# Transposing attention weights in two halves of 64 queries, first rotary sums on TensorE, and a new order, in an attention and gated feed-forward kernel

## The chip, the core and the metric

The kernel runs on one core of a Trainium2 chip. The core has TensorE (PE; its weight loads are listed apart as PEld), VectorE (DVE), ScalarE (ACT), GpSimd (POOL) and SyncE (SP, which only issues DMAs here). The metric is device time of one execution in microseconds.

## The reference

Eight batches of eight heads, 576 positions, head size 64. Queries and keys are rotated by position, softmax attention is formed, the heads are laid side by side (512 channels), and a gated feed-forward follows, whose gate is a causal convolution of five taps:

```python
def rotate(x):
    x1, x2 = (x[..., :half], x[..., half:])
    return np.concatenate([x1 * cos - x2 * sin, x1 * sin + x2 * cos], axis=-1)
q_rot, k_rot = (rotate(q), rotate(k))
scores = scale * np.matmul(q_rot, k_rot.transpose(0, 1, 3, 2))
scores = scores - np.max(scores, axis=-1, keepdims=True)
attn = np.exp(scores)
attn = attn / (np.sum(attn, axis=-1, keepdims=True) + 1e-09)
attn_out = np.matmul(attn, v)
...
for k in range(K):
    gate_pre += conv_w[k][None, None, :] * xp[:, k:k + S, :]
gate = 1.0 / (1.0 + np.exp(-gate_pre))
val = x @ w_val
return (gate * val @ w_out).astype(np.float32)
```

Everything is float32. Products that need full precision are made of three reduced ones (high times high, high times low, low times high), in the type fp32r.

## The kernel before, in words

**A pair of heads** is the unit of attention: 32 pairs, four to a batch. Head 0 lies on partitions 0 to 63, head 1 on 64 to 127. The host hands over each query and key twice, as it is and with its halves swapped. For each pair, `load` (L264) brings both copies (`kin`, `qin`); `rope_mul` (L278) multiplies each by the cosine or sine table (`tab`), `rope_add` (L283) adds them, `qk_hi` (L287) and `qk_lo` (L294) split the sum into a high part and a remainder. Keys are held 640 wide: the last 64 positions stand once more in front, so that a chunk of 128 queries can see its keys starting at either place; that wrapped part is loaded and rotated like the rest.

**Scores.** `s_mm` (L306) makes the scores of a chunk of 128 queries for both heads: twelve matmuls on 64 rows each, alternating between the upper and the lower half of the array's rows. A pair has four such chunks, and a fifth of six matmuls, which holds the last 64 queries of both heads. `s_max` (L323, DVE) takes the row maxima, `s_exp` (L328, ACT) the exponentials and their sums into `p`. Scores lie in `ps_s`, which has two places, one for each head, so that the scores of the next chunk wait for the exponentials of this one.

**Transposes.** For the product with the values, the weights `p` must be turned. `t_mm` (L355) turns, for one chunk and one head, four blocks of 128 x 128 into one bank of 512 columns of `ps_t`: a matmul with the block as the stationary operand and the identity as the moving one (`transpose`, L344). `t_copy` (L380) moves the bank to `pt` on ACT or DVE. That makes eight such banks for a pair, and some smaller ones for the remainders (keys m, h0, h1, hm: nine transposes for a pair). `pv_mm` (L406) and `pv_left` (L416) multiply by the values, into `ps_a`; `x_norm` divides by the sums.

**Feed-forward.** `f_mm` (L499) makes both projections of a batch, spread over the time in which the next batch's attention runs. The four banks of `ps_t` are shared by transposes, products with the values and projections.

**Order.** Nothing is scheduled at run time: `ORDER` lists the jobs one by one, with the engine where there is a choice (V, A, G) and the number of the buffer to use. `Plan.run` checks that no job's inputs change by the order and then issues them, so that each engine has a fixed queue. `FILLS` puts transposes of the identity, whose result nobody reads, at some places of PE's queue. The weights arrive as float64 bits; `decode` (L543) turns them into a high part and a remainder on DVE, early in the run.

Of the kernel before, what the change touches and what calls it, by code (L numbers as in the profile page):

```python
# [34 lines left out]
163 178:0 232 117 161 90 227V 164:10 225V 229G 167:1 299 165:3 168:3 91 120G 166:1 92 179V:1 93:0 169:01 125 131 230 188 94:0 170:2 95:0 182:1 172:0
196:3 171 126 128 174:0 231 173 129G 190:0 305 175:1 183A:1 197A:1 184:1 176:0 96 153 189A 233:10 300V 191A 177 185A 198:3 127 192:2 199A 200:0 234:3
194:1 193A 130G 236:2 235:3 97 237:0 307V 195A 238:10 202:1 306V 203:1 132 205:3 308G 241:0 239:1 259:2 242 180:1 301V 204:1 309 206 181A 310 240
186:1 302V 552 201A 243:01 98 303 275:0 380 187A 304G 244:3 276A:0 207:1 246:2 245:2 208 133 247:1 546 99 248:01 134 381 135 265:0 553G 251:0 209
266A:0 249:1 252 382 250 253:1 554G 210 211 138 261:0 254:3 263:3 262A:0 257:1 548V 255:0 383 258A 555V 273:0 260A 269:1 256 556 547V 312:01 270A 557
264A 267:2 214:1 279:1 549G 315:2 277:3 281:0 313:0 274A 282:0 316:3 271:0 384 631 136 314:0 215 272A 317:10 137 385 216 550 284:0 268A 386G 318:1 285  # L40
320:3 387G 319 286:2 217 388 321 283:0 551V 278A 322:10 212:1 218 280A 287 633G 325:2 625 323:0 326:2 340:3 311 389 324:1 288 390 139V 341A:1 327:01
391 140G 290 336:1 328:1 346:3 392 338:2 329 632V 339A:1 332:0 393 634G 330:3 337A 333:2 331 394 347A 356 627V 350:1 395 357A:1 342:3 626V 334:2 396V
343A 352:2 335 351A 397G 289 559:10 293:2 628V 398 348:3 353A 558 213:1 562:0 354:1 635 358:0 344:2 560:1 563:0 636 629 294 291:2 360:1 345A 399 361:1
400 561:3 585:2 710 401 630V 349A 564:01 355A 402 405 403 363:3 704 295 406G 565:3 364 362:1 292:2 567:2 566 365:1 359V 568 296 587:0 586A:0 569:01
404 588A:0 297 366 711G 570:0 572:1 571:2 583:2 407V 573:1 591:0 712V 408 298 574:01 705V 584A 592A 589:2 706G 575:3 367 577:2 576 716 368 578 579:0
369 707V 370:3 593:0 409 590A 597:3 580:0 371:3 708 601:1 595:2 594V 581:0 603:0 410 596A 709V 638:10 602A:0 604A 411 783 372:3 582 599:2 412 605:1
458:0 413 607:0 373 598A 459 608:0 415 414 460 600A 639:1 416G 606A 610:3 641:3 417G 640:3 612:2 374 418 642:1 713V 219 643:10 375 714 613 609:0 785G
644:2 646:0 645 611 715 647 662:1 419 789 614 376 663A:1 100 648:10 420 421 461:0 668:1 637 422 462 470:0 615 669A:1 463 651:1 464:3 425 423 465 652:2
784G 649:3 466 616 650:0 664:1 467:1 680:2 426V 468 653:01 424 665A 791V 681A:1 670:3 617:4 427G 656:2 476:1 671A 477 469 654:0 428 657 478 790V 655
658:1 619:4 792G 672:2 659:1 674:3 471 479:2 675A 786V 676:1 660:1 666:3 429 673A 717:01 430 661 677A 431 667A 620 678:2 793 682:1 432 684:3 472 683A  # L50
433 679A 720:3 488:1 435 489 718:2 721:3 436G 490 686:1 434 482:2 719:0 687:1 437V 483 794 438 685A 484 480 621 956 722:10 481 491:0 473:1 691:3 618:4
723:0 688:1 725:1 724 741:1 494:0 439 726 622 495 787 440 727:10 441 742A:0 788G 474 689:1 728:3 692 729:2 623 950 957G 730:2 690 485:2 731:1 693 442
486 732:10 445 443 487 694 695 743:2 475 733:0 749:1 744A 444 747:3 446G 735:1 750A 745:2 748A:0 500:1 447V 736 952V 448 751:3 501 746A 951V 737:0 734
958V 752A 496 953G 738:3 377 759:2 761:3 502 760V:0 739:0 497:2 755:2 503:1 762A 753:0 449 954 740 757:1 450 756A 763:3 796:10 451 758A 955V 765:0 498
770:2 452 766:0 698:0 799:2 499 492 797:1 771 800:3 453 959V 798:1 822:1 767:0 754V 764A 801:01 823A:1 699 504 455 768:3 505 804:0 960 1029 802:3 456G
769 805 961 803 772 454 1035 806:10 774 457G 773 777:1 493 838:0 807:2 516:1 809:1 517 808:2 506:2 700 810:0 518 839A:1 1030G 811:10 519A:1 520 824:3
814:0 795 1031G 820:0 812:3 830:1 815 507 821V 825A:1 816:0 1032V 831A 508 1036G 1033 817:2 511:0 509A:2 512 813 510 828:3 1037V 834:1 829A 1034V
826:2 818:1 513 1038G 835V 1108 526:3 827A 963:10 819 1039 840:1 964:1 832:2 514A:0 836:0 841V 833A 527 1040 965:3 528 966:0 1114 847:1 778 967:0 848
837V 1109G 529V:1 968:10 987:2 779 842:0 521:3 843A 1110G 971:3 988A:0 522 969:2 523 972 531:2 524V:2 844:1 1111G 970 532 525 533 845:1 989:0 701 515
849:3 530 990V 702 850 534A:2 846:1 780 703 973:01 1115V 696:0 624 991:0 697:0 974:1 962 775:1 993:2 976:0 851 994A:0 776:1 992V 975:2 536:2 1005:0  # L60
977:1 853 537 1116V 995:3 852 978:01 1117G 996V 854:2 856:2 997:1 979:3 538 1006A:0 855:2 981:2 980 541:3 542 982 857 983:0 539A:0 998V 543 1112 984:1
862:0 544A:1 999:2 1113V 1118 1007:1 863 1000A 858 1187 1001:3 985:0 864 1002A 545 986 1042:10 1119 1008A 1009:2 1043:0 1193 1003:3 1014:1 865:2
1044:3 781 1015 1004A 1010V 1045:3 1011:0 1016:0 1012:0 859 1046:2 535 1017 860 1120 782 1189V 1047:10 1188V 1066:3 1050:2 1190G 1068:2 1067A:1 1048:1
1018 866 1049 1013:0 868:3 1194V 869 1069A 1195G 1051 870 1070:2 1041 861 871:1 1052:10 1071V:1 872 873 1072:3 1053:0 874:2 867 1073A 1055:3 875
1054:1 1196G 1019 1084:3 876 1020 1056:0 1085V:1 1074:1 1023:3 1057:10 1075V 1021:3 877:0 1076:0 1024 880:3 1058:1 881 1060:2 882 1059 886:1 1025
1077A 1062:1 1061 883:1 1026 887 1191 1078:2 1063:0 1197 1080:0 1079V 1086:3 1064:2 888 1027 892:2 884 889:2 1081A 1121:01 1192V 890 1028 1065 1082:1
# [142 lines left out]
def attn_gated_ffn(ctx: ExitStack, tc: tile.TileContext, q2, k2, v2, tab, w_val, conv_w, w_out, out, collect=None):  # L209
# [578 lines left out]
```

## Time and profile before

| | |
|---|---|
| three runs | 743.93, 746.06, 747.79 us |
| the profiled execution | 746.22 us |
| its span in the trace | 744.4 us |
| mean granted clock of PE | 0.993 |
| matmuls | 6047 |
| PE busy, of which transposes (L349) | 718.6 us, 189.7 us |
| scores (L320) | 174.8 us, 1728 matmuls |
| row maxima (L326, DVE), 288 | 208.7 us |
| exponentials (L334, ACT), 288 | 212.7 us |

A group's busy time is the union of its instructions; a matmul's recorded duration runs over that of the next ones, so the step from one start to the next is the cost, not the duration. "Idle before" is the time an engine stood still ahead of these instructions, and behind the arrow stands what ended it.

### The profile page before, as it was taken

The numbers are of one execution on the slowest core, as the hardware profiler recorded it, in microseconds if no ns is written. First come the engines' busy times: TensorE is split into PE (matmuls) and PEld (weight loads), VectorE is DVE, ScalarE is ACT, GpSimd is POOL, SyncE is SP. The second block draws the span as 40 slices with busy tenths as digits, with TensorE's granted clock in tenths as the row PEclk, the third lists the DMA queues.
The fourth block names the chain that finished last, engine by engine and source line by source line (L and its number), as shares of the span: only waits on it lengthen the run. The fifth ranks groups of instructions, "written<-read, shape, count | busy, mean of one in ns | idle before, by whom it ended". The sixth has DMA issues, their size and how long they took to land. (4 is left out here: it accounts for less than half of the span.)

```text
span 744.4 us, 15945 instructions
## 1 busy us (share of the span) xinstructions
PE 718.6 (97%) x6047; PEld 583.5 (78%) x6047; DVE 605.3 (81%) x999; ACT 497.2 (67%) x1159; POOL 306.2 (41%) x234
## 2 busy tenths in 40 slices
PE   9897989999999999999999999999999999999998
PEld 9665656878788787877777887777878878788888
DVE  4999989998988887888888887778887878877741
ACT  1776777878676867667666876676667666776621
POOL 3344243445533614554324553454435353062121
PEclk9999899999999999999999999999999999999999
DMA  6443343234343332243432133433242243311012
GB/s 199 134 151 107 89 143 98 76 101 127 117 135 93 87 120 91 71 122 117 130 104 93 56 111 104 125 95 115 79 121 66 83 145 109 89 53 52 17 49 72
DMA packets 61167, 75.33 MB, mean 101 GB/s; under 512 B 25338, under 2 KB 35619, under 8 KB 61091
## 3 DMA queue, kind: packets, MB, share of 16 engines
q1 hardware_dynamic: 60002, 73.60, 32.6%
q8 instruction: 48, 0.79, 0.4%
q10 hardware_dynamic: 1088, 0.72, 0.4%
q14 instruction: 29, 0.23, 0.1%
HBM read 64.70 MB, written 9.59 MB: 100 GB/s over the span
## 5 line engine op out<-in xcount | busy, mean ns | idle before, releaser
L334 ACT ACTIVATE p<-ps_s,nm 128x576 f32<-128x576 f32 x288 | 212.7, 742 | 109.0 <-DVE nm L326 107.0
L326 DVE TENSOR_REDUCE nm<-ps_s 128x1 f32<-128x576 f32 x288 | 208.7, 750 | 68.8 <-PE ps_s L320 64.4
L349 PE MATMUL ps_t<-ident,p 128*128 128x128 f32 (+1 forms) x1316 | 189.7, 280 | 8.2 <-ACT pt L402 4.4
L320 PE MATMUL ps_s<-k,q 64*128 64x288 f32 (+1 forms) x1728 | 174.8, 309 | 11.4 <-ACT p L334 10.8
L349 PEld LDWEIGHTS ps_t<-ident,p 128*128 128x128 f32 (+1 forms) x1316 | 147.6, 142 | 37.6 <-issue 16.9
L320 PEld LDWEIGHTS ps_s<-k,q 64*128 64x128 f32 (+1 forms) x1728 | 136.7, 185 | 51.1 <-ACT p L334 28.2
L402 ACT COPY pt<-ps_t 128x512 f32<-128x512 f32 x203 | 116.3, 587 | 58.3 <-PE ps_t L349 57.6
L413 PE MATMUL ps_a<-pt,v 128*64 128x256 f32 (+1 forms) x1024 | 136.2, 414 | 0.3 <-ACT pt L402 0.2
L490 DVE SCALAR_TENSOR_TENSOR g<-x,cw,g 128x576 f32<-128x576 f32 (+1 forms) x132 | 118.4, 898 | 2.2 <-ACT g L487 1.5
L513 PE MATMUL ps_f<-y,wout_hi 128*128 128x288 f32 (+2 forms) x512 | 111.1, 303 | 0.0
L413 PEld LDWEIGHTS ps_a<-pt,v 128*64 128x64 f32 x1024 | 70.1, 138 | 49.9 <-issue 7.3
L528 POOL TENSOR_TENSOR y<-y,y 128x288 fp32r<-128x288 f32 (+2 forms) x64 | 56.0, 883 | 111.5 <-ACT y L525 97.4
L513 PEld LDWEIGHTS ps_f<-y,wout_hi 128*128 128x128 f32 x512 | 82.6, 188 | 5.5 <-issue 2.8
L281 POOL TENSOR_TENSOR qin<-qin,tab 128x640 f32<-128x640 f32 (+1 forms) x36 | 58.7, 1638 | 62.9 <-DMA qin<-in_q 60.5
L513 PE MATMUL ps_f<-xh,wval_hi 128*128 128x288 f32 (+2 forms) x256 | 78.2, 307 | 1.3 <-DVE pt L404 0.8
L513 PE MATMUL ps_f<-xl,wval_hi 128*128 128x288 f32 (+2 forms) x256 | 76.5, 301 | 0.0
L513 PE MATMUL ps_f<-xh,wval_lo 128*128 128x288 f32 (+2 forms) x256 | 76.3, 300 | 0.0
L513 PE MATMUL ps_f<-y,wout_lo 128*128 128x288 f32 (+2 forms) x256 | 76.1, 300 | 0.0
L281 POOL TENSOR_TENSOR kin<-kin,tab 128x640 f32<-128x640 f32 (+1 forms) x29 | 49.6, 1721 | 59.0 <-DMA kin<-in_k 58.9
L477 POOL TENSOR_TENSOR xl<-x,xh 128x576 fp32r<-128x576 f32 (+2 forms) x33 | 47.3, 1437 | 45.6 <-ACT xh L471 27.7
L404 DVE COPY pt<-ps_t 128x512 f32<-128x512 f32 x85 | 57.4, 678 | 8.0 <-PE ps_t L349 7.8
L334 ACT ACTIVATION_READ_ACCUMULATOR p<-ps_s,nm 128x1 f32 x288 | 57.2, 199 | 0.0
(70 smaller groups left out, 838.5 us busy)
## 6 DMA issues: line engine op xcount, KB each, us to landing
kin<-in_k SPq DMA_DIRECT2D x31, 576.0 KB
qin<-in_q SPq DMA_DIRECT2D x31, 512.0 KB
v<-in_v SPq DMA_DIRECT2D x32, 320.0 KB
out_t<-o SPq DMA_DIRECT2D x56, 144.0 KB
rb<-rd SPq DMA_DIRECT2D x31, 144.0 KB
rb<-rd SPq DMA_DIRECT2D x31, 128.0 KB
kin<-in_k SPq DMA_DIRECT2D x32, 64.0 KB
wst<-in_w_val SPq DMA_DIRECT2D x4, 512.0 KB
```

Source lines behind the costliest of these rows:

```text
L281: eng.tensor_tensor(out=t[:, i, a:b], in0=t[:, i, a:b], in1=table[:, i, a + at:b + at], op=ALU.mult)
L320: T.matmul(out=tiles[h][:, half, 0:288], lhsT=st["q"][rows, x, c * 128:c * 128 + 128], rhs=st["k"][rows, y, k0:k0 + 288], start=(i == 0), ...
L326: V.tensor_reduce(out=st[f"nm{i}"], in_=st[f"s{i}"], axis=AX.XY, op=ALU.max, negate=True)
L334: A.activation(out=st[f"p{t}"][:, part].rearrange("p (b x) -> p b x", b=2), in_=st[f"s{i}"], func=AF.Exp, bias=st[f"nm{i}"], scale=1.0, ac ...
L349: T.transpose(out=bank[0:src.shape[1], j * 128:(j + 1) * 128], in_=src, identity=ident)
L402: A.copy(out=dst, in_=src)
L404: V.tensor_copy(out=dst, in_=src)
L413: T.matmul(out=st[f"a{g}"][HEAD[h], 0:n], lhsT=st["v"][:, j, h, :], rhs=st[f"pt{g}"][:, h * 4 + j], start=(j == 0), stop=False)
L477: G.tensor_tensor(out=st["xl"][:, a:b], in0=xs[p % 2][:, 4 + a:4 + b], in1=st["xh"][:, a:b].bitcast(F32), op=ALU.subtract)
L490: V.scalar_tensor_tensor(out=g, in0=x_sb[:, a + k:b + k], scalar=w, in1=g, op0=ALU.mult, op1=ALU.add)
L513: T.matmul(out=acc[:, 0:n], lhsT=wt[w][:, kc, ds], rhs=mv, start=(kc == 0 and i == 0), stop=(kc == NCH - 1 and i == 2))
L528: G.tensor_tensor(out=ffn[b][1][:, dc, lo:hi], in0=ffn[b, "y", dc, lo], in1=ffn[b][0][:, dc, lo:hi].bitcast(F32), op=ALU.subtract)
```

## The change

Four things change.

1. A chunk's transposes are made in halves of 64 queries. Instead of eight matmuls of 128 x 128 (four blocks, two heads), sixteen take 64 partitions of `p` each as the stationary operand (64 rows, 128 columns) and a 64 x 64 piece of the identity as the moving one. The upper 64 queries go to bank a, the lower 64 to bank b, in turn; a bank holds both heads. Both heads' exponentials must be there first. `t_copy` empties a bank as eight pieces of 64 columns, where it had four of 128.
2. Of the first pair of heads (`RAW = 1`) only one copy of queries and keys is loaded; both table products are made of it, and PE sums them, with the identity and a swap matrix as stationary operands (`rope_mm`). High part and remainder are then taken from PSUM.
3. Keys are 576 wide in loads, table products and sums; the wrapped 64 columns are copied afterwards (`k_wrap`, ACT). The table is loaded without its wrapped parts.
4. `ORDER` and `FILLS` are new throughout: 86 filling transposes instead of 185. `decode` uses a bitwise and and a maximum in place of a comparison with a product; it has as many steps.

`CONV = 0`: a convolution on PE (`tap_mm`, `tap_gate`) is in the text and not used.

```diff
+RAW = 1
+CONV = 0
-9 8 16 15 22 0:0 101 11G 28 10G 12G 13 111 14V 18V 17G 19V 20 23V 24V 1 25V 2 21V 26 141 27 3 102 35:01 103 36:0 29G 38:1 30G 37:0 104 39:1 31V 105 32
...
-FILLS = {29: (113, 0, 'h0', 0), 41: (19, 0, 'h0', 0), 54: (19, 0, 'h0', 0), 89: (8, 0, 'h1', 3), 161: (20, 1, '7', 2), 364: (6, 3, 'h1', 2)}
+FILLS = {54: (25, 0, '2a', 1), 66: (16, 0, '0a', 2), 82: (11, 0, '3a', 1), 92: (8, 0, '1a', 0), 185: (6, 1, '1a', 3), 362: (8, 3, '1a', 2), 376: (8, 3, 'hm',
+         3), 463: (4, 4, '1a', 3)}
...
     def rope_mul(p, n, i, a, b, eng):
         t = ins[n]
-        at = 0 if n == "k" else D
-        eng.tensor_tensor(out=t[:, i, a:b], in0=t[:, i, a:b], in1=table[:, i, a + at:b + at], op=ALU.mult)
+        eng.tensor_tensor(out=t[:, i, a:b], in0=t[:, 0 if p < RAW else i, a:b], in1=table[:, i, a:b], op=ALU.mult)
...
+    def rope_mm(p, n, a, b):
+
+        bank = ring("ps_t", [128, 512], F32, "ps_r", psum)
+        state[p][f"b{n}{a}"] = bank
+        for i, m in enumerate((ident, swap.rearrange("p h i x -> p (h i x)"))):
+            T.matmul(out=bank[:, 0:b - a], lhsT=m, rhs=ins[n][:, i, a:b], start=(i == 0), stop=(i == 1))
...
+    def k_wrap(p):
+
+        t = state[p]["k"]
+        A.copy(out=t[:, :, 0:D], in_=t[:, :, S:W].bitcast(F32))
...
         else:
-            c, h = int(key) // 2, int(key) % 2
-            i = order(p).index(c)
-            x = 640 * (i % 2)
-            srcs = [flat(p, f"{i // 2}{h}")[:, x + j * 128:x + (j + 1) * 128] for j in range(4)]
+            halves(p, key)
+            return
         transpose(p, key, srcs)
+
+    def halves(p, key):
+
+        st = state[p]
+        i = order(p).index(int(key))
+        for x in "ab":
+            if "b" + key + x not in st:
+                st["b" + key + x] = ring("ps_t", [128, 512], F32, "ps_t", psum)
+        for h in range(2):
+            f = flat(p, f"{i // 2}{h}")
+            for j in range(4):
+                at, to = 640 * (i % 2) + j * 128, (h * 4 + j) * D
+                for x, rows in zip("ab", HEAD):
+                    T.transpose(out=st["b" + key + x][:, to:to + D], in_=f[rows, at:at + 128], identity=ident[rows, rows])
...
-            src = bank.rearrange("p (j x) -> p j x", j=4)
-            dst = turned(p, g)[:, h * 4:h * 4 + 4, (c - 2 * g) * 128:(c - 2 * g) * 128 + 128]
+            at = (c - 2 * g) * 128 + "ab".index(key[1]) * D
+            src = bank.rearrange("p (s x) -> p s x", x=D)
+            dst = turned(p, g)[:, :, at:at + D]
...
-            lambda: V.tensor_scalar(out=wa, in0=hi, scalar1=0x07FFFFFF, scalar2=3, op0=ALU.bitwise_and,
-                                    op1=ALU.logical_shift_left),
+            lambda: V.tensor_scalar(out=wa, in0=hi, scalar1=0x7FFFFFFF, scalar2=None, op0=ALU.bitwise_and),
+            lambda: V.tensor_scalar(out=fa, in0=fa, scalar1=2.0 ** -15 * 1.125, scalar2=None, op0=ALU.max),
+            lambda: V.tensor_scalar(out=wa, in0=wa, scalar1=0x07FFFFFF, scalar2=3, op0=ALU.bitwise_and, op1=ALU.logical_shift_left),
             lambda: V.scalar_tensor_tensor(out=wa, in0=hi, scalar=-0x40000000, in1=wa, op0=ALU.bitwise_and, op1=ALU.bitwise_or),
-            lambda: V.tensor_scalar(out=hi, in0=hi, scalar1=0x7FF00000, scalar2=None, op0=ALU.bitwise_and),
-            lambda: V.scalar_tensor_tensor(out=fa, in0=hi, scalar=float(0x38100000), in1=fa, op0=ALU.is_ge, op1=ALU.mult),
```

The order itself is best seen as each engine's queue. First PE in the middle of the run, in the thirteenth pair of heads, before: `ps_s` rows are scores, `ps_t<-ident,p` transposes, `ps_a` products with the values (`pt` with the four blocks, `pr` with the remainders).

```order
L320 MATMUL ps_s<-k_70,q_72 128x288 x12
L413 MATMUL ps_a<-pt_3428,v_76 64x256 x4
L413 MATMUL ps_a<-pt_3372,v_76 64x320 x4
L413 MATMUL ps_a<-pt_3428,v_76 64x256 x4
L413 MATMUL ps_a<-pt_3372,v_76 64x320 x4
L320 MATMUL ps_s<-k_70,q_72 128x288 x12
L349 MATMUL ps_t<-ident,p 128x128 x4
```

The same place in the same pair after it, where `128x64 x16` is one chunk in halves:

```order
L332 MATMUL ps_s<-k_71,q_73 128x288 x12
L395 MATMUL ps_t<-ident,p 128x64 x16
L438 MATMUL ps_a<-pt_3704,v_77 64x256 x8
L438 MATMUL ps_a<-pt_3637,v_77 64x320 x4
L332 MATMUL ps_s<-k_71,q_73 128x288 x12
L395 MATMUL ps_t<-ident,p 128x64 x16
L438 MATMUL ps_a<-pt_3637,v_77 64x320 x4
```

A chunk's whole set of transposes now stands directly behind a chunk's scores, in one piece, and the products with the values are moved behind it. Next, PE at the start of the program, before:

```order
L342 MATMUL ps_t<-ident 128x128 x113
L320 MATMUL ps_s<-k_70,q_72 128x288 x12
L342 MATMUL ps_t<-ident 128x128 x19
L320 MATMUL ps_s<-k_70,q_72 128x288 x12
L342 MATMUL ps_t<-ident 128x128 x19
L320 MATMUL ps_s<-k_70,q_72 128x288 x12
```

and after, where `ps_r` rows are the rotary sums of the first pair:

```order
L287 MATMUL ps_r<-kin,ident 128x288
L287 MATMUL ps_r<-kin,swap 128x288
L287 MATMUL ps_r<-kin,ident 128x288
L287 MATMUL ps_r<-kin,swap 128x288
L287 MATMUL ps_r<-qin,ident 128x384
L287 MATMUL ps_r<-qin,swap 128x384
L287 MATMUL ps_r<-qin,ident 128x256
L287 MATMUL ps_r<-qin,swap 128x256
L332 MATMUL ps_s<-k_71,q_73 128x288 x12
L354 MATMUL ps_t<-ident 128x128 x25
```

The 113 fillers ahead of the first scores are gone, and eight float32 matmuls stand there. ACT at the same place, before:

```order
L262 DMA tab<-in_tab 128x2x64
L262 DMA tab<-in_tab 128x2x256
L594 ACT_TABLE_LOAD
L594 ACTIVATE warm<-x_83 128x1
L262 DMA tab<-in_tab 128x2x320
L262 DMA tab<-in_tab 128x2x64
```

and after:

```order
L640 ACT_TABLE_LOAD
L640 ACTIVATE swap<-ident 128x2x32 x2
L633 DMA tab<-in_tab 128x2x288
L635 ACTIVATE warm<-x_84 128x1
L633 DMA tab<-in_tab 128x2x288
```

The first load of the rotary table moved behind the load of ACT's function table and the making of the swap matrix.

More of the change, by code (lines that the diff above doesn't have):

```diff
@@ L35 @@
[L35 to L42, printed above, removed]
@@ L239, in attn_gated_ffn @@
     ident = const.tile([128, 128], F32, name="ident")
-    table = const.tile([128, 2, W + D], F32, name="tab")
-    ins = {n: const.tile([128, 2, W], F32, name=f"{n}in") for n in "kq"}
+    wide = {"k": S, "q": W}
+    swap = const.tile([128, 2, 2, HALF], F32, name="swap")
+    table = const.tile([128, 2, W], F32, name="tab")
+    ins = {n: const.tile([128, 2, wide[n]], F32, name=f"{n}in") for n in "kq"}
     parts = {n: [const.tile([128, 2, W], F32R, name=f"{n}{i}") for i in range(2)] for n in "kq"}
@@ L271, in load @@
             if x < y:
-                SP.dma_start(out=t[rows, :, x:y], in_=q2[p, rows, :, x - off:y - off])
+                SP.dma_start(out=t[rows, i, x:y], in_=q2[p, rows, i, x - off:y - off])
     def load_v(p):
@@ L495, in gate, with tap_diag, tap_mm, tap_gate @@
         A.activation(out=g, in_=g, func=AF.Tanh, scale=0.5)
+    def tap_diag(p):
+        t = state[p]["dg"] = ring("wst", [128, TAPS, 128], F32, "dg")
+        for k in range(TAPS):
+            i = p % PPB * TAPS + k
+            A.activation(out=t[:, k], in_=ident, func=AF.Copy, scale=cw[:, i:i + 1])
+    def tap_mm(p, a, b):
+        bank = state[p][f"bg{a}"] = ring("ps_t", [128, 512], F32, "ps_g", psum)
+        for k in range(TAPS):
+            T.matmul(out=bank[:, 0:b - a], lhsT=state[p]["dg"][:, k], rhs=xs[p % 2][:, a + k:b + k], start=(k == 0), stop=(k == TAPS - 1))
+    def tap_gate(p, a, b):
+        st = state[p]
+        if "g" not in st:
+            st["g"] = ring("pg", [128, S], F32, "g")
+        A.activation(out=st["g"][:, a:b], in_=st[f"bg{a}"][:, 0:b - a], func=AF.Tanh, scale=0.5)
     ffn = {}
@@ L591, in load_tab, with make_swap, tab_wrap @@
     def load_tab(a, b):
-        around(table, tab[0], a, b, A)
+        A.dma_start(out=table[:, :, a:b], in_=tab[0, :, :, a:b])
         if a == 0:
             A.activation(out=warm, in_=xs[0][:, 0:1], func=AF.Exp)
+    def make_swap():
+        t = ident.rearrange("p (h i x) -> p h i x", h=2, i=2)
+        for i in range(2):
+            A.activation(out=swap[:, :, i], in_=t[:, :, 1 - i], func=AF.Copy, scale=-1.0)
+    def tab_wrap():
+        A.copy(out=table[:, :, S:W], in_=table[:, :, 512:S])
     if collect is None:
@@ L661, in attn_gated_ffn @@
             else:
-                i = order(p).index(int(key) // 2)
-                r = f"p/{p}.{i // 2}{int(key) % 2}#{key}"
-            b = f"ps_t/{p}{key}"
-            add("P", t_mm, p, key, r=r, w=b)
-            add("VA", t_copy, p, key, r=b, w=f"pr/{p}#{key}" if g == "r" else f"pt{g}/{p}#{key}")
+                i = order(p).index(int(key))
+                r = " ".join(f"p/{p}.{i // 2}{h}#{2 * int(key) + h}" for h in R2)
+            banks = [key + x for x in "ab"] if key.isdigit() else [key]
+            add("P", t_mm, p, key, r=r, w=" ".join(f"ps_t/{p}{x}" for x in banks))
+            for x in banks:
+                add("VA", t_copy, p, x, r=f"ps_t/{p}{x}", w=f"pr/{p}#{x}" if g == "r" else f"pt{g}/{p}#{x}")
         cols = {None: range(9), 0: (0, 1, 2, 3), 1: range(4, 9)}
@@ L675, in attn_gated_ffn @@
         for g in R2:
-            keys = [str(i) for i in range(4 * g, 4 * g + 4)] + ["m"] * g
+            keys = [f"{c}{x}" for c in (2 * g, 2 * g + 1) for x in "ab"] + ["m"] * g
             r = toks(f"pt{g}/{p}#@", keys) + f" v{p % 3}"
```

318 lines of the change are left out of this document (173 added, 145 removed).

## The prediction

> **What bounds the kernel now.** The page comes first: how busy each engine is, and how that is spread over the run. The two digit rows are 40 slices of 18.6 us.
>
> ```profile
> span 744.4 us, 15945 instructions
> PE 718.6 (97%) x6047; PEld 583.5 (78%) x6047; DVE 605.3 (81%) x999; ACT 497.2 (67%) x1159; POOL 306.2 (41%) x234
> PE   9897989999999999999999999999999999999998
> DVE  4999989998988887888888887778887878877741
> ```
>
> TensorE is close to full on average, but not everywhere: in the first ten slices VectorE carries the higher digits. So the run is read in stretches next. I cut at 185 us and 681 us, where the ninth and the last pair of heads begin; the first view is busy time of all engines, the second that of the probability transposes (L349), the third that of the row maxima (L326, nine for a pair).
>
> ```profile
> 17.00:185.00 168.00, 151.44 (x1237) 114.77 (x1235) 156.90 (x270) 124.68 (x293) 71.02 (x53) 0.97 0.38 113
> 185.00:681.00 496.00, 491.32 (x4220) 399.82 (x4219) 410.49 (x653) 344.15 (x800) 215.06 (x153) 1.00 0.33 99
> 681.00:744.00 63.00, 60.19 (x480) 53.47 (x480) 31.24 (x60) 25.44 (x63) 13.86 (x16) 1.00 0.17 56
> 185.00:681.00 496.00, 136.37 (x947) 105.44 (x947) 1.00 0.33 99
> 17.00:185.00 168.00, 51.66 (x72) 0.97 0.38 113
> 185.00:681.00 496.00, 150.51 (x207) 1.00 0.33 99
> ```
>
> The columns are PE, PEld, DVE, ACT, POOL, then granted clock. From 17 to 185 us (72 maxima, 8 pairs) DVE is busy 156.9 of 168 us (93%) and PE idles 17 us: DVE sets the pace. From 185 to 681 us (207 maxima, 23 pairs) PE is busy 491.3 of 496 us while DVE has 83%: **PE alone bounds two thirds of the run**. The last 63 us are PE again, mostly the closing projections. What PE waits for in all is small:
>
> ```profile
> PE ps_s L320 <- ACT p L334: 10.8, 18, 3.3
> PE ps_t L349 <- ACT pt L402: 4.4, 4, 2.8
> ```
>
> **The transposes: the main term.** The costliest PE group is the one that is changed; 23 pairs issue 947 of these in the middle stretch, 41 for a pair, and the change halves 32 of each 41. What one costs is read from an undisturbed row of 19, since these matmuls overlap: start to last start.
>
> ```profile
> L349 PE MATMUL ps_t<-ident,p 128*128 128x128 f32 x1284 | 185.4, 280 | 8.2 <-ACT pt L402 4.4 <-DVE x L464 1.1 <-ACT pr L402 1.0
> 17.58 2.29 PE L342 MATMUL ps_t<-ident 128*128 128x128 f32 x19
> 303.93 0.88 PE L349 MATMUL ps_t<-ident,p 128*128 128x128 f32 x6
> 303.93 0.20 PEld L349 LDWEIGHTS ps_t<-ident,p 128*128 128x128 f32 x2 [0.16 <-issue]
> 302.94 0.19 PEld L320 LDWEIGHTS ps_s<-k,q 64*128 64x128 f32 x2 [0.49 <-ACT y L525]
> 302.94 1.06 PE L320 MATMUL ps_s<-k,q 64*128 64x288 f32 x12
> ```
>
> Nineteen take 2.29 us; less the last one's own 0.27 that is 2.02 us for 18 steps, 0.11 us each with a slower first one. I use **109 ns** per whole transpose. It moves 128 columns. A half moves 64 on one half of the array's rows, and two halves make one whole: 32 pairs of halves for a pair of heads.
>
> What a pair of halves costs isn't in the trace, so it is bounded. Below: if moving columns set it, half of 109, 55 ns. The weight load gives a bound near that: in the row with x2, two loads span 0.20 us and one lasts 0.14, so the second starts 0.06 us after the first: 59 to 61 ns. Above: if the two halves shared nothing, 2 x 55 = 110 ns, so nothing gained. Between these decides whether the halves run at once. The score rows do the same with the same split (64*128): their two first loads span 0.19 us and each lasts 0.18, so both row halves load within 0.01 us; and twelve matmuls of 288 columns have 0.77 us between first and last start (1.06 less 0.29), six steps for twelve matmuls. Row halves do run side by side. I take **62 ns**, the load's step, nearest row to the case, and keep 55 to 110.
>
> The saving is 109 - 62 = 47 ns. In the middle stretch, 23 x 32 x 47 ns = **-34.6 us**. In the last stretch one pair: 32 x 47 ns = **-1.5 us**. In the first stretch I take **0**: PE already idles 17 us there and DVE does not get less to do soon (below). Bounds there -6 to +5.
>
> A rule of the Trainium skill speaks against this. "TensorE: Matmul & The Clock Gate", section "LDWEIGHTS (loading the stationary operand)", says that a weight load costs its columns over 1.2 GHz whatever the number of rows, so 107 ns for a half as for a whole; by it a pair would stay near 109 ns and the middle term would be 0. The 0.06 us step in the row above disagrees; its consequence stands among the rivals.
>
> **Mode changes.** Each change of array split costs PE: 303.93 is the first transpose after score matmuls. Its six span 0.88 us, less 0.27 that is 0.61 for five steps instead of 0.545, and the score row's last start (302.94 + 0.77 = 303.71) lies 0.22 us before. So some 0.1 to 0.2 us a change. Halves have the scores' split, so changes between these two go; changes between halves and projections come. Counted in the order of before and after: 345 and 351. Six more: +1 us at most, inside the next term.
>
> **What gives back.** With PE faster by 1.5 us a pair (496 / 23 = 21.6 us now), the next limit is nearer. DVE: the key work is 576 wide instead of 640, and jobs move between engines.
>
> ```profile
> L281 DVE TENSOR_TENSOR kin<-kin,tab 128x640 f32<-128x640 f32 x36 | 34.4, 970 | 2.1 <-DMA kin<-in_k 2.0
> L300 DVE TENSOR_TENSOR k<-kin,k 128x640 fp32r<-128x640 f32 x21 | 17.2, 819 | 0.8 <-ACT k L292 0.6
> L404 DVE COPY pt<-ps_t 128x512 f32<-128x512 f32 x85 | 57.4, 678 | 8.0 <-PE ps_t L349 7.8
> L402 ACT COPY pt<-ps_t 128x512 f32<-128x512 f32 x203 | 116.3, 587 | 58.3 <-PE ps_t L349 57.6
> ```
>
> By its row, 36 key products at 970 ns become 30 at a tenth less (-8.7 us), 21 remainders lose a tenth (-1.7), two copies go (-1.4); query products go from 28 to 32 (+4): about -8 us in all, -6 in the middle stretch, so 404 us. Against 461 us that is 88%, under the 93% of the first stretch, where PE idled a tenth. Between 83% (PE idle 1%) and 93% (10%) I take 1.5% more idle: **+7 us**, bounds 0 to +18. In it is the wait for banks: both banks of a chunk now fill at once, and on ACT the second copy follows 0.59 us later; the scores and projections queued behind cover it on PE, and without cover the 4.4 us wait for L402 could double. The wrapped 64 key columns become a copy on ACT, 32 small ones; ACT has 152 us idle in the middle (496 - 344), and it is hidden there. Two decode steps change kind, not number: nothing.
>
> **The start.** The first scores start at 16.59 us; the first query product on DVE at 11.09 us waited for loads.
>
> ```profile
> 16.59 1.06 PE L320 MATMUL ps_s<-k,q 64*128 64x288 f32 x12
> 11.09 1.02 DVE L281 TENSOR_TENSOR qin<-qin,tab 128x384 f32<-128x384 f32 x2
> 2.07 1.28 ACT L594 ACT_TABLE_LOAD   x1 [2.07 <-issue]
> 0.00:17.00 17.00, 15.64 (x119) 15.48 (x121) 6.65 (x17) 2.93 (x5) 6.25 (x12) 1.00 0.70 214
> ```
>
> Ahead of the first queries' product came, by their shapes (128 x columns x 4 bytes), 704 KB of keys, 704 KB of tables and 384 KB of queries; now 288, 576 and 192 KB. At the 214 GB/s of the first 17 us the 736 KB less are 3.5 us. Against it: the sums move to PE, in four float32 groups that stand ahead of the first scores and run on a PE that no filler has warmed, and on ACT the first load of the rotary table now stands behind the load of the function table (1.28 us). I take **-2 us**, bounds -5 to +2.
>
> **Sum.** 744.4 - 2 + 0 - 34.6 + 7 - 1.5 = 713.3 us of span. The profiled execution took 746.2 us, 1.8 more than its span, and it agrees with the median of the three runs, 746.06. So 713.3 + 1.8 = **715 us**, 4% faster.
>
> **Rivals.**
> - The load isn't hidden: each pair of halves waits some 20 ns more for its weights, 82 ns. Middle 23 x 32 x 27 = -20 us, wait +3, start and end -3: 726 us. For: load step and column time are nearly equal, so neither hides the other. Against: whole transposes step at 109 with no visible extra. Chance 0.12.
> - DVE and the softmax chain become the bound: DVE can't be driven past its 83% because each chunk goes scores, maximum, exponential, next scores. 404 / 0.83 = 487, so -9 in the middle, -3 elsewhere: 734 us. For: ACT waits 107 us for maxima. Against: 93% in the first stretch. Chance 0.11.
>
> ```profile
> ACT p L334 <- DVE nm L326: 107.0, 82, 5.2
> L349 PEldq EVENT_SEMAPHORE  x1: 51/51/51, 576.4 to 576.4; - x1
> L320 PEldq EVENT_SEMAPHORE  x2: 51/51/51, 576.7 to 578.3; - x2
> 576.83 0.38 PE L513 MATMUL ps_f<-xh,wval_hi 128*128 128x288 f32 x1
> 578.89 0.29 PE L513 MATMUL ps_f<-xh,wval_lo 128*128 128x288 f32 x1
> 579.11 1.06 PE L320 MATMUL ps_s<-k,q 64*128 64x288 f32 x12
> ```
>
> - The halves don't do what they are for: a half's load lasts as long as two, pair 107 to 110 ns. Middle 0, start -2: 744 us, no change. Against: the 0.06 us step. Chance 0.07.
> - **Slower: instructions come too slowly.** A pair of halves is two loads and two matmuls instead of one of each. The densest long stretch in the trace, the twelve scores, passes a matmul each 64 to 70 ns. If that is the sequencer's pace, a pair costs 128 ns, 19 more than now: 23 x 32 x 19 = +14 us, less the start: 758 us. It decides from 27 ns an instruction. Against: the sequencer itself leaves rows (PEldq). It stood at the transposes' wait at 576.4 and at that of the scores of 579.11 already at 576.7; between lie the projections of 576.83 to 578.89, 16 matmuls with their loads, 32 instructions in 0.3 us, some 10 ns each. Chance 0.05. The Trainium skill, "TensorE: Matmul & The Clock Gate", section "Wait — 56ns, not 53.3ns?", has such a pace: about 62 ns per matmul when decoding runs in firmware. By it a pair costs 124 ns and the sum would be some 755 us; the two semaphore rows disagree.
>
> **How the numbers follow.** Forecast 715 us with 0.65; rivals 726 (0.12), 734 (0.11), 744 (0.07), 758 (0.05). The forecast's own spread, from its bounds (wait 0 to 18, start -5 to +2, first stretch -6 to +5, pair 56 to 66 ns), is about 700 to 728. The range takes in 726 and most of the 734 case: 698 to 735, leaving out 0.12 for the last two and some at the ends. Half a per cent, 3.7 us, is about what a measurement of this kernel can tell from no change. Faster by more: 0.65 + 0.12 + 0.11 = 0.88; within: 0.07; slower: 0.05.
>
> **What would show it.** In the new profile: sixteen halves in a row should take about 8 x 62 ns plus one matmul's own time, some 0.75 us; 1.1 us or more means the third or fourth rival. PE's busy time should fall by 45 to 50 us. In the middle stretch PE should stay above 95% busy; if it idles a tenth while DVE is at 85% or less, the second rival holds. The first scores should start near 14.5 us. The forecast is wrong if halves don't overlap, or if the new order makes PE wait for maxima more than 18 us longer.

## The result, and the profile after

The kernel after takes **711.93 us** (median of four runs, 708.45 to 713.98) against 744.99 us for the kernel before (median of four): a ratio of 0.955, 95% interval 0.950 to 0.960. The prediction was 715 us, range 698 to 735. In the experiments the kernel after came to 708.87 us, median of six (ratio 0.952, 0.948 to 0.956). The profiled execution took 708.45 us, with a span of 706.6, the shortest of the first four. The ratios given here and below leave out one run of whole (870.37 us, at a granted clock of 0.753) and two of tap_twice (815.92 us at 0.747 and 747.38 us at 0.974), which the medians in the table take in.

The page of after: span, busy time by engine, and three digit rows, now in slices of 17.7 us.

```profile
span 706.6 us, 17745 instructions
PE 673.5 (95%) x6988; PEld 539.6 (76%) x6988; DVE 592.5 (84%) x995; ACT 502.7 (71%) x1197; POOL 298.9 (42%) x231
PE   5888988899999999999999999999999999999998
DVE  4989998998899888899879988898888888887731
PEclk9988998999999999999999999999999999999999
```

PE lost 45 us of busy time, DVE 13, the span 38. The same three stretches as before the change: the cuts are where the ninth and the last pair of heads begin, now 181.1 and 643.8 us. The columns are PE, PEld, DVE, ACT, POOL, granted clock; the fourth row is the halves (L395) alone.

```profile
14.00:181.00 167.00, 149.44 (x1518) 112.07 (x1519) 157.04 (x284) 123.82 (x297) 69.19 (x51) 0.94 0.36 111
181.00:644.00 463.00, 458.81 (x4955) 371.82 (x4951) 402.27 (x641) 349.37 (x830) 213.60 (x156) 1.00 0.34 104
644.00:707.00 63.00, 58.77 (x510) 51.46 (x508) 28.80 (x57) 26.05 (x64) 13.13 (x15) 1.00 0.18 56
181.00:644.00 463.00, 64.72 (x1482) 58.32 (x1476) 1.00 0.34 104
```

Read against the rows of before, the gain sits in one row. The middle went from 496 to 463 us, with PE still at 99% of it. The first eight pairs went from 168 to 167, the last stretch stays at 63. Within the middle, all transposes (L349: the 32 of a pair that were changed, and the nine that were not) held 136.4 us of PE; now the halves hold 64.7 and the nine (L361, 209 in the middle) 37.2, together 99.9 since they overlap a little. PE's busy time fell by the forecast's 45 to 50 us (45.1).

What a pair of halves costs is read from an undisturbed row of sixteen in the timeline of after (start, span, count):

```profile
301.49 0.71 PE L395 MATMUL ps_t<-ident,p 64*128 64x64 f32 x16
```

Its group of instructions, with busy time, mean of one, and the idle time before them:

```profile
L395 PE MATMUL ps_t<-ident,p 64*128 64x64 f32 x2048 | 94.6, 228 | 6.2 <-DVE x L489 2.3 <-ACT pt L427 1.0 <-ACT pr L427 0.8
```

And two of its waits (us in total, times, longest):

```profile
PE ps_s L332 <- ACT p L346: 10.6, 20, 1.5
ACT p L346 <- DVE nm L338: 72.8, 73, 3.6
```

Sixteen halves take 0.71 us; less the last one's own 0.22 that is 0.49 for seven pairs' steps, the first of them longer: in the list of starts behind this row the later pairs step at 62 ns and the two of a pair start 3 to 4 ns apart. Over the whole run, PE's wait for the copies ahead of these transposes did not double but fell (4.4 to 1.0 us), that for exponentials is what it was (10.6 against 10.8), and ACT's for maxima fell from 107.0 to 72.8.

### The profile page after: what moved, and what is told of

The parts are those of the page before. It is cut to its first block, busy times and chain, and to the rows that moved or that the text cites. A ratio compares the mean times of both kernels' runs of the same rounds, so it can differ in the third digit from the quotient of the medians.

```text
span 706.6 us, 17745 instructions
## 1 busy us (share of the span) xinstructions
PE 673.5 (95%) x6988; PEld 539.6 (76%) x6988; DVE 592.5 (84%) x995; ACT 502.7 (71%) x1197; POOL 298.9 (42%) x231
## 4 chain that ended last, share of the span: by engine, by line
PE 74%; DVE 14%; ACT 7%; issue 2%; DMA 1%; SPq 1%; POOL 0%; DVEq 0%; ACTq 0%
PE ps_f L555 27%; PE ps_s L332 18%; PE ps_a L438 13%; PE ps_t L395 8%; PE ps_t L361 5%; DVE g L515 4%; DVE nm L338 4%; ACT p L346 3%; PE ps_a L448 3%; ACT pt L427 2%; DVE q L304 1%; PE ps_r L287 1%; DMA rb<-rd 1%; DVE y L563 1%; DVE wst L594 0%
## 5 line engine op out<-in xcount | busy, mean ns | idle before, releaser
L346 ACT ACTIVATE p<-ps_s,nm 128x576 f32<-128x576 f32 x288 | 213.1, 744 | 74.3 <-DVE nm L338 72.8
L332 PE MATMUL ps_s<-k,q 64*128 64x288 f32 (+1 forms) x1728 | 180.6, 312 | 11.1 <-ACT p L346 10.6
L332 PEld LDWEIGHTS ps_s<-k,q 64*128 64x128 f32 (+1 forms) x1728 | 141.6, 188 | 40.4 <-ACT p L346 24.6
L438 PE MATMUL ps_a<-pt,v 128*64 128x256 f32 (+1 forms) x1024 | 140.8, 415 | 2.1 <-DVE y L563 1.2
L515 DVE SCALAR_TENSOR_TENSOR g<-x,cw,g 128x576 f32<-128x576 f32 (+1 forms) x132 | 121.4, 922 | 1.4 <-ACT g L512 0.8
L555 PE MATMUL ps_f<-y,wout_hi 128*128 128x288 f32 (+2 forms) x512 | 108.1, 302 | 0.0
L438 PEld LDWEIGHTS ps_a<-pt,v 128*64 128x64 f32 x1024 | 67.4, 137 | 47.8 <-issue 5.5
L395 PEld LDWEIGHTS ps_t<-ident,p 64*128 64x128 f32 x2048 | 83.4, 141 | 24.9 <-issue 7.8
L276 POOL TENSOR_TENSOR kin<-kin,tab 128x576 f32<-128x576 f32 (+1 forms) x33 | 52.5, 1598 | 116.2 <-DMA kin<-in_k 88.4
L395 PE MATMUL ps_t<-ident,p 64*128 64x64 f32 x2048 | 94.6, 228 | 6.2 <-DVE x L489 2.3
L276 POOL TENSOR_TENSOR qin<-qin,tab 128x640 f32<-128x640 f32 (+1 forms) x32 | 51.8, 1628 | 37.0 <-DMA qin<-in_q 17.9
```

The source lines that it names most:

```text
L276: eng.tensor_tensor(out=t[:, i, a:b], in0=t[:, 0 if p < RAW else i, a:b], in1=table[:, i, a:b], op=ALU.mult)
L332: T.matmul(out=tiles[h][:, half, 0:288], lhsT=st["q"][rows, x, c * 128:c * 128 + 128], rhs=st["k"][rows, y, k0:k0 + 288], start=(i == 0), ...
L346: A.activation(out=st[f"p{t}"][:, part].rearrange("p (b x) -> p b x", b=2), in_=st[f"s{i}"], func=AF.Exp, bias=st[f"nm{i}"], scale=1.0, ac ...
L395: T.transpose(out=st["b" + key + x][:, to:to + D], in_=f[rows, at:at + 128], identity=ident[rows, rows])
L438: T.matmul(out=st[f"a{g}"][HEAD[h], 0:n], lhsT=st["v"][:, j, h, :], rhs=st[f"pt{g}"][:, h * 4 + j], start=(j == 0), stop=False)
L515: V.scalar_tensor_tensor(out=g, in0=x_sb[:, a + k:b + k], scalar=w, in1=g, op0=ALU.mult, op1=ALU.add)
```

## The experiments

Ten runs, all of the kernel after or of an edit of it. Ratios are to the kernel before, run on the same chip.

| run | what differs from after | median us | ratio, 95% |
|---|---|---|---|
| whole | transposes whole again | 746.19 | 1.001 (0.998 to 1.004) |
| in_turn | halves of one side, then of the other | 731.24 | 0.984 (0.978 to 0.989) |
| warm | 28 fillers ahead of the first sums | 708.41 | 0.951 (0.945 to 0.957) |
| tap | fifth tap left out | 702.50 | 0.943 (0.938 to 0.948) |
| tap_twice | fifth tap added twice | 741.61 | 0.997 (0.993 to 1.000) |
| less_pe | a third of the value projection left out | 699.19 | 0.942 (0.937 to 0.947) |
| both | tap and less_pe | 687.65 | 0.923 (0.918 to 0.927) |
| again | nothing | 708.87 | 0.952 (0.948 to 0.956) |
| warm_again | as warm | 708.25 | 0.951 (0.947 to 0.956) |
| shapes | rows of matmuls of one kind each, ahead of the first sums | 759.58, one run | |

### Are the halves the whole gain?

The first run keeps the new order, the rotary sums on TensorE and every other part, and only makes a chunk's transposes whole again (the two banks then hold a head each, and the copies take four runs of 128 instead of eight of 64):

```diff
-                for x, rows in zip("ab", HEAD):
-                    T.transpose(out=st["b" + key + x][:, to:to + D], in_=f[rows, at:at + 128], identity=ident[rows, rows])
+                T.transpose(out=st["b" + key + "ab"[h]][:, j * 128:j * 128 + 128], in_=f[:, at:at + 128], identity=ident)
...
```

> The kernel after with its own order, but each chunk's transposes whole again (128 by 128, eight a chunk where there were sixteen halves); the two banks then hold one head's columns each. Theory (the halves alone bring the gain): a whole costs 109 ns where two halves cost 62, so 47 ns on each of 736 pairs in the 23 pairs of heads of the middle, 34.6 us, and 1.5 us in the last; in this order 392 changes of array split stand where 351 did, 41 more at 0.1 to 0.2 us, 4 to 8 us; in the first eight pairs 0 to 5 us. Sum 40 to 49 us on 712: 752 to 761 us, slower than the kernel before by 1 to 2%. Rival (the new order and the rotary sums on TensorE bring part of it, and the halves only the rest): under 745 us, and as low as 725 if they bring most.

It measured 746.19 us. The lower bound of the first theory was 752, so the 41 extra changes of split (a change of split: a matmul that uses the array's rows or columns in other pieces than the one ahead of it) did not show; but it is level with the kernel before, against the rival, that the new order brings part of the gain. The middle of this kernel, and its whole transposes alone:

```profile
13.90:182.80 168.90, 153.05 (x1266) 114.71 (x1265) 158.27 (x284) 124.60 (x297) 67.45 (x51) 0.99 0.34 109
182.80:679.40 496.60, 494.62 (x4208) 397.04 (x4207) 403.89 (x640) 350.64 (x828) 214.11 (x157) 1.00 0.31 96
182.80:679.40 496.60, 98.97 (x737) 80.24 (x736) 1.00 0.31 96
```

With VectorE's work as in after (404 us there, 402 in after), the middle takes 496.6 us, 0.7 more than before the change (680.9 - 185.0 = 495.9 by the pairs' starts) and 33.9 more than after (643.8 - 181.1 = 462.7). 736 whole transposes at 47 ns are 34.6 us. How far one profile can be trusted is seen in again, the kernel after unchanged:

```profile
180.10:644.50 464.40, 458.95 (x4951) 371.22 (x4947) 403.29 (x640) 348.94 (x829) 213.92 (x156) 1.00 0.33 103
```

Its middle is 1.7 us longer than after's, and those of warm and warm_again, which have the same queue there, take 465.2 and 465.7 us. So the 33.9 us stand for 31 to 34. **In this order the halves are the whole gain, and what else was changed, as it stands in whole, is worth nothing that can be measured.** Two things are not separated. Whole has 41 changes of split more than the kernel before; at the 145 ns measured below, they could hide up to 6 us that the new order brings. And halves in the old order were not run.

### Why a half is cheap: the side, or the size?

The second run issues eight halves of the upper rows and then eight of the lower:

```diff
-        for h in range(2):
-            f = flat(p, f"{i // 2}{h}")
-            for j in range(4):
-                at, to = 640 * (i % 2) + j * 128, (h * 4 + j) * D
-                for x, rows in zip("ab", HEAD):
+        for x, rows in zip("ab", HEAD):
+            for h in range(2):
+                f = flat(p, f"{i // 2}{h}")
+                for j in range(4):
+                    at, to = 640 * (i % 2) + j * 128, (h * 4 + j) * D
```

> The kernel after, but a chunk's sixteen halves run eight on the upper rows first and then eight on the lower, so that neighbours share their rows. Theory (two halves run at the same time because neighbours are on different rows): a half then takes 55 to 62 ns by itself, a pair 110 to 124 where it took 62, 48 to 62 ns on each of 768 pairs in the middle and the end, 37 to 48 us, less what the bank of the first eight halves being ready earlier gives (0 to 5 us): 745 to 760 us, and sixteen halves in a row take 1.8 to 2.1 us. Rival (a half is cheap by itself, the row side does not matter): 31 ns a half as now, 712 us, sixteen in 0.75 us.

731.24 us: 19 more than after, where 37 to 48 was expected, and not 0, the rival's. Its row of sixteen in the timeline, at the place of the row of after:

```profile
302.25 0.96 PE L395 MATMUL ps_t<-ident,p 64*128 64x64 f32 x16
```

Its middle, by windows:

```profile
180.90:664.00 483.10, 481.01 (x4950) 396.20 (x4946) 405.82 (x640) 350.39 (x829) 213.09 (x156) 1.00 0.32 99
```

Sixteen take 0.96 us, 0.25 more than alternating. For 92 chunks of the middle that is 23 us, and the middle is 20.4 longer. So neighbours on one side do cost more, but only half of what I worked out. (The 1.8 to 2.1 us expected for the row were a slip besides: eight pairs at the expected 110 to 124 ns, and the last one's own 0.22, are 1.1 to 1.2 us.) The single starts behind that row show why: the upper ones step at 55 to 64 ns, the first lower one starts at 302.50 us, and the last three upper ones, earlier in the program, start only at 302.55, 302.62 and 302.68. TensorE lets the other side go ahead of the program's order by that much. Three steps of 62 ns are the 0.19 us by which the row is shorter than sixteen halves one after the other (15 x 62 ns and 0.22 us, 1.15).

The next run measures the step of each kind by itself, in rows of 24 ahead of the first rotary sums (`up` is rows 0 to 63, `low` the others):

```diff
...
+        for _ in range(24):
+            one(a, up)
+        for _ in range(12):
+            one(a, up)
+            one(b, low)
+        for _ in range(24):
+            one(a, up, slice(0, 64))
...
+        for _ in range(24):
+            one(a, every, slice(0, 64))
+        for _ in range(12):
+            one(a, every)
+            one(a, up)
...
```

> The kernel after with 360 matmuls more ahead of the first rotary sums, in a dozen rows of 24 of one kind each, for their steps alone; the total says nothing. Whole transposes step at 109 ns and alternating halves at 62 ns a pair, as in the kernels. Theory (a half's 62 ns is its weight load of 128 columns, since in the run with the halves in turn the halves of one side stepped at 62 ns each, not at 55): loads of 64 columns step at about 55 ns, the time of 64 moved columns, or less; moving 32 columns under loads of 128 still steps at about 62 ns. Rival (the moved columns set the step): loads of 64 columns change nothing, and 32 moved columns step at 28 to 35 ns. Alternating sides doubles the rate in every kind. A whole and a half in turns step at 85 ns on average if a change of split costs nothing, at 150 or more if each costs 0.1 us.

Pieces from the timeline of that run, in this order: whole; upper halves alone; halves alternating; upper halves that load 64 columns; those alternating; whole ones that load 64 columns; a whole and an upper half in turns (the row names the form of its first).

```profile
12.10 0.82 PE L355 MATMUL ps_t<-ident 128*128 128x128 f32 x6
13.30 1.23 PE L355 MATMUL ps_t<-ident 64*128 64x64 f32 x17
14.44 0.91 PE L355 MATMUL ps_t<-ident 64*128 64x64 f32 x22
15.44 1.22 PE L355 MATMUL ps_t<-ident 64*64 64x64 f32 x19
16.65 0.74 PE L355 MATMUL ps_t<-ident 64*64 64x64 f32 x20
17.73 2.46 PE L355 MATMUL ps_t<-ident 128*64 128x128 f32 x21
20.34 3.03 PE L355 MATMUL ps_t<-ident 64*128 64x64 f32 x13
```

Each span, less the last one's own 0.22 (a half) or 0.27 (a whole), over its steps. Whole: 0.55 / 5 = 110 ns. Upper alone: 1.01 / 16 = 63. Alternating: 0.69 for 21 steps, 66 ns a pair, so twice the rate. Loading 64 columns: 1.00 / 18 = 56 alone, 55 a pair alternating. A whole that loads 64 columns: 2.19 / 20 = 109. So a whole's step is its 128 moved columns; a half's is the load of 128 columns, 62 to 63 ns, with the 64 moved columns right behind at 56. The theory holds as far as it was tried: loads of 64 columns brought the step from 63 to 56 ns, where the rival had no change. (These halves also write 64 partitions where the others write 128, which is not separated from the load.) The moves of 32 columns were not transposes but full float32 products, 112 ns each, so that part of the rival was not tried. The last kind: 12 steps in 2.76 us, 230 ns each where (109 + 63) / 2 = 86 would be free: a change of split costs some 145 ns.

The Trainium skill, "TensorE: Matmul & The Clock Gate", section "LDWEIGHTS (loading the stationary operand)", has the load go by columns and not by rows. The trace agrees: on 64 rows the step is 63 ns for 128 columns and 56 or less for 64, and two loads of 128 rows and 128 columns, in the prediction's row with x2, start 0.06 us apart. It does not agree with 107 ns, the estimate for 128 columns by the section's rule, neither by the step, 63 ns, nor by the recorded length of one load, 0.14 us.

### Is the start on the path?

The rotary sums of the first pair ran at the half clock until about 12.3 us, because nothing ran ahead of them. The edit puts 28 identity transposes there:

```diff
-FILLS = {54: (25, 0, '2a', 1), 66:
+FILLS = {15: (28, 0, 'x', 3), 54: (25, 0, '2a', 1), 66:
```

> The kernel after with 28 whole identity transposes more ahead of the first rotary sums, on a TensorE that waits there for loads anyway. Theory: the sums L287 run at the half clock from 7.5 to about 12.3 us since nothing ran ahead of them; warmed, their eight rows take 0.6 us each, the first scores start at 11.9 to 12.5 us instead of 14.1, and the time falls by 1.5 to 2.5 us if the start is in the path. Rival: the first eight pairs are paced by VectorE at 89 to 90% busy, which starts its work at the same time, so the end does not move: 0 us. Second rival: the query products at 10.5 us wait for the table copy on ScalarE, so the first scores move by under 0.8 us.

> The kernel after once more, unchanged, beside the next run on the same chip: 708 to 714 us.

> The kernel after with the 28 identity transposes ahead of the first rotary sums, once more, beside the kernel after on the same chip. Theory (the start is on the path): first scores at 11.5 us instead of 14.1 and 2 to 3 us less in the median. Rival (VectorE's pace in the first eight pairs takes it back): within 1 us of the kernel after.

The first sum and the first scores of after, then the same two of warm, from their timelines:

```profile
7.52 1.33 PE L287 MATMUL ps_r<-kin,ident 128*128 128x288 f32 x2 [7.52 <-POOL kin L276]
14.08 0.40 PE L332 MATMUL ps_s<-k,q 64*128 64x288 f32 x2
```

```profile
6.97 0.65 PE L287 MATMUL ps_r<-kin,ident 128*128 128x288 f32 x2
11.45 0.40 PE L332 MATMUL ps_s<-k,q 64*128 64x288 f32 x2
```

A sum of 288 columns takes half as long, and the scores come 2.6 us earlier, as expected; the second rival (the table copy on ACT) is out. What it is worth at the end stays open: 3.5 us less in the first comparison, 0.6 us in the second, on one chip. All ten runs of each taken together differ by 1.9 us in the mean (710.2 and 708.3), with each kernel's runs spread over 7 to 8 us. That is nothing that these runs can tell from no change; a 95% interval of the difference goes from none to some 4 us.

The four profiles show where it is lost. The ninth pair begins at 177.8 us in warm and 176.5 in warm_again, against 181.1 in after and 180.1 in again, so the first eight pairs pass the earlier start on, and the first rival, that VectorE's pace there takes it back, does not fit. But the middle, with the same queue, took 465.2 and 465.7 us against 462.7 and 464.4. Why is open.

### What bounds the kernel now?

The prediction had +7 us for what VectorE gives back, with bounds 0 to 18, and after shows 1 to 4 us of it. Four kernels take VectorE's or TensorE's load down or up. The fifth convolution tap is a VectorE instruction per pair; a third of the value projection is 256 matmuls:

```diff
-        else:
+        elif k < TAPS - 1:
             g = st["g"][:, a:b]
             V.scalar_tensor_tensor(out=g, in0=x_sb[:, a + k:b + k], scalar=w, in1=g, op0=ALU.mult, op1=ALU.add)
```

(tap_twice instead repeats the last line once where `k == TAPS - 1`) and

```diff
+            if stage == 0 and i == 2:
+                continue
...
```

The lines left out here mark the last matmul of a sum one place earlier.

> The kernel after without the fifth tap of the convolution over time (its instructions on VectorE are left out, about 30 us of VectorE's 592; that part of the output is missing a term). Theory (after the change TensorE is still the only bound of the middle, 458.8 of 463 us busy, and VectorE bounds only the first eight pairs): the middle gains no more than 3 us of its 4.2 us of idle TensorE, the first eight pairs up to 7 us of their 17.6: 702 to 711 us. Rival (VectorE and the chain of maximum and exponential pace the middle already): 30 us less of VectorE brings 15 us or more, under 697 us.

> The kernel after with the fifth convolution tap added twice (so that part of the output is wrong by that term): about 26 us more on VectorE, 19 of them in the middle, which goes from 402 to 421 of 463 us there (91%). Theory of the prediction (TensorE's idle time follows VectorE's share, 1% idle at 83%, 10% at 93%): 8% idle, some 35 us more in the middle, about 745 us. Rival (in the middle the order leaves VectorE's work off TensorE's path up to that share): at most 5 us in the middle and 5 to 6 us in the first eight pairs, 715 to 723 us.

> The kernel after without the value projection's products with the low part of the weights (256 matmuls of 128 by 288 left out, so the output lacks that small term): about 256 times 133 ns = 34 us less on TensorE, some 25 us of it in the middle, 3 in the first eight pairs, 6 in the last pair. Theory (TensorE is still the only bound of the middle): 678 to 686 us; VectorE then has 92% there. Theory of the prediction (TensorE's idle time follows VectorE's share): the middle gives back most, over 700 us. Between them, 686 to 700 us, the chain of scores, maximum and exponential, 20 us a pair, takes over.

> The kernel after with both cuts at once: without the value projection's products with the low part of the weights (34 us of TensorE) and without the fifth convolution tap (26 us of VectorE; the output lacks both terms). Either cut alone left the middle within 2 to 6 us of its 463. Theory A (VectorE's work is what lies just under TensorE's: with either cut alone the other engine holds the time): the middle falls to some 440 us, the whole to 672 to 684 us. Theory B (the chain from scores to maximum to exponential to the next scores, some 20 us a pair, holds the middle whatever VectorE's other work is): the middle stays above 452 us, the whole above 690 us.

The middle of each, in the order tap, tap_twice, less_pe, both (columns as above):

```profile
177.60:638.60 461.00, 457.50 (x4950) 371.04 (x4945) 383.54 (x617) 348.05 (x829) 209.06 (x156) 1.00 0.33 104
```

```profile
188.40:677.80 489.40, 466.89 (x4951) 374.90 (x4947) 434.27 (x663) 348.98 (x829) 217.02 (x156) 0.99 0.31 98
```

```profile
180.60:637.70 457.10, 444.57 (x4761) 350.67 (x4758) 403.61 (x639) 348.00 (x828) 215.15 (x156) 1.00 0.34 105
```

```profile
176.70:627.60 450.90, 441.86 (x4757) 349.81 (x4755) 376.78 (x616) 347.07 (x828) 210.55 (x156) 1.00 0.34 106
```

Against after's 462.7 us, with PE busy 458.8 and DVE 402.3:

| run | PE busy in the middle | DVE busy there | length of the middle |
|---|---|---|---|
| again | +0.1 | +1.0 | +1.7 |
| whole | +35.8 | +1.6 | +33.9 |
| tap | -1.3 | -18.7 | -1.7 |
| tap_twice | +8.1 | +32.0 | +26.7 |
| less_pe | -14.2 | +1.3 | -5.6 |
| both | -16.9 | -25.5 | -11.8 |

More work on either engine lengthens the middle by most of what is added; less on one of them alone brings little, in tap no more than again differs by. The kernel after stands **in a corner**: TensorE sets the time, and the other side, VectorE and the chain of scores, maximum and exponential, lies some 6 to 9 us under it (457.1 us in less_pe, 462.7 to 465.7 in the four profiles with after's middle). DVE is idle for 60 us of the middle, yet when it got 32 us more, the middle grew by 26.7. The clock of that row is 0.99 and not 1.00: three spells of half clock lie in it, 3.4 us each, where after's middle has none. By an estimate, half of that time, 5 us, is the most that they cost TensorE, so VectorE took 5 to 10 of the 32 us without time. By the ratios, 0.997 against 0.952 to 0.955, the whole run took 31 to 33 us longer. PE's wait for exponentials says the same. Over the whole run it was 10.6 us in after; here it is in tap_twice, then in less_pe:

```profile
PE ps_s L332 <- ACT p L346: 21.4, 27, 2.2
```

```profile
PE ps_s L332 <- ACT p L346: 19.2, 39, 1.5
```

In the middle alone this wait is 1.7 us in after, 9.1 in tap_twice and 8.0 in less_pe.

Against what was expected: tap, 702.50 us, is at the edge of what "TensorE alone bounds the middle" gave, 702 to 711. Its first eight pairs took 162.8 us with 4 to 5 us less of DVE, where the four profiles of after, again, warm and warm_again have 165.1 to 167.0, so VectorE sets the pace there at least in part (the half clock differs too: 13.7 us of it in tap, as in warm_again with 165.1, and 20.5 in after). tap_twice, 741.61 us, is near the 745 of the prediction's theory and far from the rival's 723. The nearness is luck: PE idled 5% of the middle (22.5 of 489.4 us) and not 8, and DVE got 44 us in all (592.5 to 637.0) where I had counted 26. The added instructions' group in tap_twice:

```profile
L517 DVE SCALAR_TENSOR_TENSOR g<-x,cw,g 128x576 f32<-128x576 f32 (+2 forms) x33 | 37.2, 1127 | 1.2
```

They took 1127 ns each, 37 us, where leaving the tap out had saved 26. less_pe, 699.19 us, falls between its two theories, where the chain had been expected to take over: 190 matmuls fewer in the middle (4951 in again, 4761 here) are 25 us by their steps and 14 in busy time, and the middle fell by 5.6. both, 687.65 us, falls between A and B: taking 25.5 us from VectorE, worth 1.7 us alone, is worth 6.2 once PE has less to do, so its work is part of that lower floor; whether the rest of it is the chain's length or the order of the instructions isn't settled.

## Why the prediction held, step by step

- **TensorE alone bounds the middle: right, but with less room than said.** Most of the gain came there, 33.2 of 37.8 us of span, and the 34.6 us of 736 x 47 ns stand against a measured 33.9 us (whole against after) and 33.2 (before against after); with the other three profiles of this middle, against 30 to 32. The rivals of a slower pair are out: the row of sixteen took 0.71 us, where 0.75 was forecast, 82 ns a pair would have given 0.8 and 107 over 0.95. The pace of instructions is no bound either: a half every 31 ns.
- **62 ns a pair, the load's step: right, for the reason given.** The load of 128 columns takes longer than the 64 moved columns, by 7 ns (63 against 56 in shapes).
- **The give-back of +7 us: mis-sized.** By the pairs' starts, the middle fell by 33.2 where 34.6 - 7 = 27.6 was forecast, so 1.4 came back; by whole against after 0.7; over all four profiles of this middle 1 to 4. The step that failed is "between 83% (PE idle 1%) and 93% (10%) I take 1.5% more idle": DVE's share came out as said (402 us, 87%, against 404 and 88%), but PE's idle time does not grow evenly with it: 1 to 4 us came back at 87%, and beyond that most of what was added.
- **The rival "DVE and the softmax chain become the bound", 734 us: a real limit at the wrong place.** I put its floor at 487 us in the middle, from DVE's 83% as a ceiling. less_pe ran the middle in 457 us, with DVE at 88%. After lies 6 to 9 us above that.
- **The start, -2: right in size (16.59 to 14.08 us, 2.5), less in what it is worth.** warm shows that 2.6 us more are lost there to the half clock, as the prediction had reckoned against it, without a size; it also shows that of earlier first scores little reaches the end of the program.
- **First stretch 0, last -1.5: near.** 168.4 to 167.0 us by the pairs' starts, inside the bounds of -6 to +5, and 63.5 to 62.8, half of what was forecast.
- **Mode changes, "+1 us at most": not seen.** One costs 145 ns by itself, inside the 0.1 to 0.2 us that was read from before. Six of them would be 0.9 us. That the 41 of whole, 6 us, did not show as time is not explained.
- **The new order, the narrower keys, the moved loads: nothing together,** as whole's 1.001 shows (but for up to 6 us that its changes of split may hide). The narrower keys and moved jobs had been put at -8 us of DVE work; DVE's busy time fell by 13 (10 in whole) and bought no time that shows.

The sum: start -2.5, first stretch -1.4, middle -33.2, last stretch -0.7, together -37.8 us of span in the profiled executions (744.4 to 706.6), against -31.1 forecast. The medians moved by 33.1, since the profiled execution of after was the shortest of its four.

## What to carry to other kernels

Two matmuls on different halves of the array's rows run at once, so a transpose that is cut at 64 rows and alternated between the halves costs little more than half; order them alternately, since eight of one side in a row give back half of the gain. Before counting on the next saving on the same engine, take some work off it and see how far the time follows: here 190 matmuls fewer, 25 us by their steps, brought 6 to 9. And a busy share below 100% is no measure of slack, the time that can be added without cost: VectorE idled 60 us and had 5 to 10 to give.

## What the runs showed of the hardware that was not expected

- **The other half of the array goes ahead of the program.** In in_turn, in the row at 302.25 us, the lower halves began while three upper ones, earlier in the program, had not started. The Trainium skill, "TensorE: Matmul & The Clock Gate", section "The mechanism", has matmuls start and end strictly in order; the starts in this trace differ.
- **The half clock comes in spells of 3.4 us or a multiple of it, also where the records show no pause between matmuls.** After has three of 6.8 us, all in the first eight pairs; again has five of 3.4 us there, tap one of 3.4 and one of 10.2. Two of after's are in these windows (columns as above: the clock is 0.54 and 0.53 over 7 us):

```profile
32.00:39.00 7.00, 6.47 (x36) 4.39 (x33) 6.30 (x15) 6.29 (x16) 2.16 (x2) 0.54 0.48 161
67.00:74.00 7.00, 5.89 (x47) 4.29 (x43) 6.77 (x12) 5.14 (x13) 2.85 (x2) 0.53 0.40 131
```

  In shapes one of 6.8 us began at 23.4 us, while wholes and halves followed each other in turns without a gap, and one of 23.9 us at 33.6, among the products that move 32 columns; two windows around the first (PE, granted clock):

```profile
20.40:23.20 2.80, 2.80 (x14) 1.00 0.02 6
24.10:27.00 2.90, 2.90 (x9) 0.50 0.00 0
```

  What starts them and what they cost is not shown. The first eight pairs took 167.0 us in after at a mean clock of 0.94 and 168.9 in whole at 0.99, but whole has 3.6 us more of TensorE's work there. Of one kernel's runs those at the higher clock tend to be the shorter: warm took 703.56 us at 0.995 and 711.85 at 0.985. That is a connection, not a cause that was tried, and it has exceptions: again took 711.40 us at 0.990 and 709.08 at 0.988.
